# Attention stages of a float32 pipeline: normalisation and all later stages one slot later

## Chip, cores and metric

One NeuronCore of a Trainium2 chip runs the kernel. The metric is the time of one execution on the device, in microseconds (us). The engines go by their short names: PE (TensorE), PEld (its weight loads), DVE (VectorE), ACT (ScalarE), POOL (GpSimd), SP (SyncE, here a queue of DMA issues). Each executes its own instructions in order and waits on semaphores for the others.

## The reference

Attention in chunks, then two gated feed-forward blocks without a nonlinearity, all in float32:

```python
for c in range(nc):                                  # 24 chunks of 32 queries
    k_full = concat(mem_k, k[l_start:r_end])         # 8 memory keys + 16 left, 32, 8 right
    scores = scale * q_c @ k_full.T
    a = exp(scores - max(scores))
    a = a / (sum(a) + 1e-9)
    out[c] = a @ concat(mem_v, v[l_start:r_end])
x = out.reshape(3072, 512)
x = ((x @ w1) * (x @ w2) @ w3) @ w_out               # 512 -> 1024 -> 512
return (x @ w_a) * (x @ w_b) @ w_out2                # 512 -> 1536 -> 512
```

There are 4 batches, 8 heads, 768 positions and a head size of 64. The weights arrive as 64-bit numbers and are turned into float32 on the chip.

## The kernel before

**Phases.** The program has three phases. Up to about 107 us (the weight phase), PE multiplies w3 by w_out once (tile `wps`), while ACT scales and DVE assembles each weight block from its 64-bit halves: `w_scale` (L361, L362 on ACT), then `w_bits` (L366, L367, L368 on DVE; tiles `w3f`, `wo_f`, `dec`). Up to about 560 us (the main loop) PE runs the first block over six tiles of 512 tokens: `psA`, `psB` (x times w1 and w2), then `psY`. After that comes the second block in a form with seven products (`ps`, `ops`). A float32 operand of a large product is split in a high and a low part (L140 on ACT writes the high, L143 on DVE the low one).

**Attention** runs beside the first two phases, in 64 units of 96 queries and 4 heads. A unit passes through eight stages: `a_scores` (PE, tile `sc` in PSUM), `a_max` (DVE: masking or the row maximum, L182, and its negation, L183; from unit 22 on L186 and L190, which also read `sc` from PSUM), `a_exp` (ACT, four exponentials with their sums, L205), `a_norm` (DVE L216 and L217 for the reciprocal of the sums, then POOL L218, the product in place in `t`), `a_trans` (PE, tile `pt`), `a_pt` (ACT L230), `a_pv` (PE, `xp`, for two units at once), `a_x` (ACT L140 and DVE L143 into `xt`, the x of the main loop).

**The order** is written by hand. A slot is a call of `attn_slot`; each unit starts three slots after the last. `STAGES` gives each stage its slot after the unit's start and the order within a slot. Behind the stages of a slot the q and k of a later unit are loaded by SP (`a_load`), and for units from 22 on split (`a_prep_hi` on ACT, `a_prep_lo` on DVE). In the weight phase the slots stand between the products, together with `w_step`, which puts a weight block through one step on ACT and DVE and issues the next load on SP. In the main loop `between` (L627) issues slots after each group of 12 products, so many that `NEED[ti]` slots are done when tile ti begins; `NEED` is the slot count by which the x of a tile is complete. SP's queue therefore holds weight loads (`raw`) and q, k and v loads in one line; a weight load waits until DVE has read the block that had its buffer.

Of the kernel before, what the change touches and what calls it, by code (L numbers as in the profile page):

```python
# [17 lines left out]
GQ = 96  # L18
# [3 lines left out]
TT = 512  # L22
NT1 = B * S // TT
NU = B * NG * 2
# [20 lines left out]
def tile_attention_moe(  # L45
# [204 lines left out]
    def a_x(u):  # L250
# [18 lines left out]


    STAGES = (
        (8, a_x),
        (7, a_pv),
        (6, a_pt),
        (5, a_trans),
        (3, a_norm),
        (2, a_exp),
        (1, a_max),
        (0, a_scores),
    )  # L280
    acount = [-3]
    NSLOT = 3 * (NU - 1) + 9

    NEED = [3 * (2 * -(-TT * (i + 1) // GQ) - 1) + 9 for i in range(NT1)]

    def attn_slot(n=1):
        for _ in range(n):
            s = acount[0]
            if s >= NSLOT:
                return  # L290
            acount[0] += 1
            for off, stage_of in STAGES:
                u, r = divmod(s - off, 3)
                if r == 0 and 0 <= u < NU:
                    stage_of(u)

            if s % 3 == 0 and s // 3 + 1 > NPLAIN + 1:
                a_prep_lo(s // 3 + 1)
            if s % 3 == 2 and s // 3 + 2 > NPLAIN + 1:
                a_prep_hi(s // 3 + 2)  # L300
            if s % 3 == 0 and NPLAIN <= s // 3 + 1 <= NPLAIN + 1:
                a_prep_hi(s // 3 + 1)
            if s % 3 == 1 and NPLAIN <= s // 3 + 1 <= NPLAIN + 1:
                a_prep_lo(s // 3 + 1)
            if s % 3 == 2:
                if s // 3 + 2 <= NPLAIN + 1:
                    a_load(s // 3 + 2)
                if s // 3 + 3 >= NPLAIN + 2:
                    a_load(s // 3 + 3)
            if s % 3 == 1 and s // 3 > 2:  # L310
                a_v(s // 3 - 1)
# [315 lines left out]
    def between():  # L627
# [10 lines left out]
        if ti < NT1 - 1:  # L638
            b = nstep[0] - NB * ti
            attn_slot(NEED[ti] + (NEED[ti + 1] - NEED[ti]) * b // NB - acount[0])  # L640

# [49 lines left out]
    for ti in range(NT1):  # L691
        last = ti == NT1 - 1
        gs = {}
        attn_slot(NEED[ti] - acount[0])
        if last:
# [18 lines left out]
        for n in (0, 2, 1, 3) if last else range(KD):  # L714
            psY = psd.tile([P, 512], F32, tag="d", name="psY")
            i = 0
# [284 lines left out]
```

## Time and profile before

| | us |
|---|---|
| median of 3 runs | 1130.52 |
| lowest and highest run | 1129.53, 1133.06 |
| span of the profiled execution, first to last instruction | 1132.1 |
| PE busy | 1098.0 |
| DVE busy | 647.7 |
| ACT busy | 516.5 |
| POOL busy | 286.1 |

The profiled execution leaves no time of its own beside its span, which is 1.6 us above the median of the runs. Busy times are of that execution. PE is the engine to watch: the other engines matter where PE waits for them. A wait of PE is printed in brackets behind the instruction that ended it, with the releaser that the profile infers.

### The profile page before, as it was taken

To read this page: it belongs to the slowest core of one execution; us is meant where nothing else is said; L and a number is where in the kernel's file an instruction comes from. 1 tells how busy PE (TensorE), PEld (TensorE's weight loads), DVE (VectorE), ACT (ScalarE), POOL (GpSimd) and SP (SyncE) were. 2 spreads that over 40 slices of the span, in tenths; PEclk is the share of its full clock that TensorE was granted. 3 is DMA by queue.
4 is the path that set the end of the run, shared out by engine and by line. 5 is a ranking of instruction groups with operands and counts; after the bars stand their busy time and mean duration, and the time that the engine had idled before them with its cause. 6 is when DMAs were issued, how large, how long until landed. Compare 5 with 4: busy or idle time off the path is not lost.

```text
span 1132.1 us, 15601 instructions
## 1 busy us (share of the span) xinstructions
PE 1098.0 (97%) x5344; PEld 876.0 (77%) x5344; DVE 647.7 (57%) x1374; ACT 516.5 (46%) x1321; POOL 286.1 (25%) x265
## 2 busy tenths in 40 slices
PE   4999999999999999999999999999999999999998
PEld 2555778888787888887887778888888888888887
DVE  5887956887997887874766455253222234232220
ACT  4776755666666666654544443232222223222210
POOL 1111231332332332331204223302223211233210
PEclk9989999999999999999999999999999999999999
DMA  9863535445345445335446553443434451434311
GB/s 276 236 198 124 167 109 162 127 154 173 118 158 178 130 137 188 125 105 196 166 177 219 214 191 149 171 136 134 164 130 148 177 176 66 167 134 182 140 38 37
DMA packets 65540, 174.78 MB, mean 154 GB/s; under 512 B 8152, under 2 KB 20726, under 8 KB 60854
## 3 DMA queue, kind: packets, MB, share of 16 engines
q1 hardware_dynamic: 54647, 107.45, 29.2%
q0 software_dynamic: 10528, 66.08, 15.8%
q8 instruction: 42, 0.69, 0.2%
q14 instruction: 36, 0.29, 0.1%
q10 hardware_dynamic: 287, 0.27, 0.1%
HBM read 140.20 MB, written 33.55 MB: 153 GB/s over the span
## 4 chain that ended last, share of the span: by engine, by line
PE 81%; DVE 3%; issue 2%; ACT 2%; DMA 1%; POOL 1%; DVEq 0%; ACTq 0%; POOLq 0%; SPq 0%
PE ps L787 29%; PE ops L93 17%; PE psA L93 11%; PE psB L93 10%; PE psY L93 10%; PE sc L93 2%; PE xp L93 2%; PE pt L226 1%; ACT t L205 1%; POOL t L218 0%; DVE dec L367 0%; DMA wc<-co 0%; DVE dec L368 0%; DMA vraw<-in_vw 0%; DVE xt L143 0%
## 5 line engine op out<-in xcount | busy, mean ns | idle before, releaser
L787 PE MATMUL ps<-x,w 128*128 128x512 f32 x1512 | 349.5, 390 | 3.2 <-ACT tmp L799 3.2
L787 PEld LDWEIGHTS ps<-x,w 128*128 128x128 f32 x1512 | 283.4, 188 | 64.0 <-ACT tmp L799 5.3
L804 DVE TENSOR_TENSOR tmp<-ps,tmp 128x512 f32<-128x512 f32 x108 | 74.6, 691 | 245.4 <-PE ps L787 241.3
L93 PE MATMUL psA<-xt,w 128*128 128x512 f32 x576 | 145.6, 400 | 2.8 <-ACT xt L140 1.9
L93 PE MATMUL psB<-xt,w 128*128 128x512 f32 x576 | 141.0, 393 | 0.0
L93 PE MATMUL psY<-g,wo 128*128 128x512 f32 x576 | 139.0, 393 | 0.0
L218 POOL TENSOR_TENSOR t<-t,sm 96x512 f32<-96x512 f32 x64 | 81.6, 1275 | 214.5 <-DVE sm L217 116.9
L686 POOL DMA_DIRECT2D w<-wc x72 | 39.5, 552 | 368.4 <-PE ps L787 368.3
L799 ACT ACTIVATE tmp<-ps 128x512 f32<-128x512 f32 x108 | 64.6, 598 | 147.2 <-PE ps L787 119.4
L93 PEld LDWEIGHTS psA<-xt,w 128*128 128x128 f32 x576 | 106.2, 189 | 27.4 <-ACT xt L140 3.1
L93 PEld LDWEIGHTS psY<-g,wo 128*128 128x128 f32 x576 | 105.6, 188 | 21.0
L93 PEld LDWEIGHTS psB<-xt,w 128*128 128x128 f32 x576 | 105.5, 188 | 21.0
L93 PE MATMUL ops<-wo,g 128*128 128x512 f32 x504 | 118.6, 389 | 0.0
L621 POOL TENSOR_TENSOR g<-gv,g 128x512 fp32r<-128x512 f32 x48 | 67.9, 1414 | 190.6 <-ACT g L620 171.8
L93 PEld LDWEIGHTS ops<-wo,g 128*128 128x128 f32 x504 | 94.6, 188 | 19.6
L810 ACT ACTIVATE g<-tmp 128x512 fp32r<-128x512 f32 x66 | 40.7, 633 | 130.1 <-DVE tmp L809 130.1
L811 POOL TENSOR_TENSOR g<-tmp,g 128x512 fp32r<-128x512 f32 x66 | 87.4, 1339 | 26.6 <-ACT g L810 25.7
L93 PE MATMUL wps<-wo_f,w3f 128*128 128x512 f32 x128 | 66.0, 649 | 10.3 <-DVE wo_f L368 10.3
L205 ACT ACTIVATE t<-t,mx 96x128 f32<-96x128 f32 x168 | 65.0, 390 | 14.7 <-DVE mx L190 14.7
L93 PE MATMUL ops<-fo,g 128*128 128x512 f32 x288 | 68.2, 389 | 0.0
L620 ACT ACTIVATE g<-gv 128x512 fp32r<-128x512 f32 x48 | 30.2, 629 | 71.4 <-DVE gv L619 71.4
L93 PEld LDWEIGHTS ops<-fo,g 128*128 128x128 f32 x288 | 54.1, 188 | 11.2
(79 smaller groups left out, 1298.8 us busy)
## 6 DMA issues: line engine op xcount, KB each, us to landing
w<-wc POOLq DMA_DIRECT2D x36, 1024.0 KB, 6.6
w<-wc POOLq DMA_DIRECT2D x36, 768.0 KB, 4.6
wc<-co SPq DMA_DIRECT2D x84, 256.0 KB, 2.5
raw<-in_wab SPq DMA_DIRECT2D x24, 512.0 KB, 3.6
kraw<-in_kt SPq DMA_DIRECT2D x42, 256.0 KB, 2.9
raw<-in_w3a SPq DMA_DIRECT2D x16, 512.0 KB, 8.3
vraw<-in_vw SPq DMA_DIRECT2D x64, 128.0 KB, 3.2
raw<-in_w SPq DMA_DIRECT2D x16, 512.0 KB, 3.4
```

The source lines that it names most:

```text
L93: nc.tensor.matmul(o, lhsT=l, rhs=r, start=first, stop=last)
L205: nc.scalar.activation(t[:, h, :], src[:, h, :], AF.Exp, bias=mx[:, h : h + 1], scale=scale, accum_out=sm[:, h : h + 1],)
L218: nc.gpsimd.tensor_tensor(t, t, sm[:, :, None].to_broadcast([GQ, HH, KW]), ALU.mult)
L226: nc.tensor.transpose(pt[:, h, :], t[:, h, :], id_sb)
L620: nc.scalar.activation(g2[:, 0, :], gv, AF.Copy)
L621: nc.gpsimd.tensor_tensor(g2[:, 1, :], gv, g2[:, 0, :].bitcast(F32), ALU.subtract)
L686: nc.gpsimd.dma_start(out=t[:, c0:c1].bitcast(F32), in_=src[:, c0:c1])
L787: nc.tensor.matmul(ps, lhsT=w[:, i, a, k, :], rhs=xs[i][:, b, k, :], start=first and n == 0, stop=n == 5, skip_group_check=not first,)
L799: nc.scalar.activation(z, ps, AF.Copy)
L804: nc.vector.tensor_tensor(z, ps, y, ALU.add)
L810: nc.scalar.activation(g2[:, 0, :], z, AF.Copy)
L811: nc.gpsimd.tensor_tensor(g2[:, 1, :], z, g2[:, 0, :].bitcast(F32), ALU.subtract)
```

## The change

Five of the eight stages get a slot number that is one higher: x 9, PV 8, the copy of the transposes 7, the transposes 6 and normalisation 4. Exponentials, masking and scores keep 2, 1 and 0. Slots that are equal modulo 3 meet in one slot, so normalisation of a unit now stands directly ahead of the masking of the next one (it stood ahead of the next unit's scores, a slot earlier), the transposes ahead of the scores, and x in the slot after the exponentials, no longer ahead of them in the same slot. The total of slots and `NEED` grow by one.

```diff
     STAGES = (
-        (8, a_x),
...
+        (9, a_x),
...
-        (3, a_norm),
+        (4, a_norm),
         (2, a_exp),
...
-    NSLOT = 3 * (NU - 1) + 9
+    NSLOT = 3 * (NU - 1) + 10
...
-    NEED = [3 * (2 * -(-TT * (i + 1) // GQ) - 1) + 9 for i in range(NT1)]
+    NEED = [3 * (2 * -(-TT * (i + 1) // GQ) - 1) + 10 for i in range(NT1)]
```

On DVE in the weight phase, around the normalisation of unit 0 (`sm_204`) and the masking of unit 1 (`mx_242`), before:

```order
L366 TENSOR_SCALAR w3f_216<-raw64_148 128x512
L367 SCALAR_TENSOR_TENSOR w3f_216<-raw64_148,w3f_216 128x512
L368 ISA w3f_216<-raw64_148,w3f_216 128x1024
L216 TENSOR_SCALAR sm_204<-sm_204 96x4
L217 RECIPROCAL sm_204<-sm_204 96x4
L366 TENSOR_SCALAR wo_f_150<-raw64_156 128x512
L367 SCALAR_TENSOR_TENSOR wo_f_150<-raw64_156,wo_f_150 128x512
L368 ISA wo_f_150<-raw64_156,wo_f_150 128x1024
L182 TENSOR_REDUCE mx_242<-sc_227 96x4
L183 TENSOR_SCALAR mx_242<-mx_242 96x4
```

and in the change, where `sc_224` is the same scores tile:

```order
L366 TENSOR_SCALAR wo_f_150<-raw64_156 128x512
L367 SCALAR_TENSOR_TENSOR wo_f_150<-raw64_156,wo_f_150 128x512
L368 ISA wo_f_150<-raw64_156,wo_f_150 128x1024
L216 TENSOR_SCALAR sm_204<-sm_204 96x4
L217 RECIPROCAL sm_204<-sm_204 96x4
L182 TENSOR_REDUCE mx_242<-sc_224 96x4
L183 TENSOR_SCALAR mx_242<-mx_242 96x4
```

The reciprocal, which releases POOL's product, has moved behind a weight block and directly ahead of the masking.

On ACT in the weight phase, around the exponentials of unit 3 and the first x (`xt`), before and in the change:

```order
L230 ACTIVATE p2_314<-pt_293 128x384
L361 ACTIVATE raw64_222<-raw64_222 128x512
L362 ACTIVATE raw64_222<-raw64_222 128x512
L140 ACTIVATE xt_349<-xp_333 128x4x96
L205 ACTIVATE t_342,sm_344<-sc_319,mx_343 96x128 x4
L361 ACTIVATE raw64_239<-raw64_239 128x512
L362 ACTIVATE raw64_239<-raw64_239 128x512
```

```order
L230 ACTIVATE p2_328<-pt_309 128x384
L205 ACTIVATE t_333,sm_335<-sc_314,mx_334 96x128 x4
L361 ACTIVATE raw64_236<-raw64_236 128x512
L362 ACTIVATE raw64_236<-raw64_236 128x512
L140 ACTIVATE xt_365<-xp_340 128x4x96
```

The high part of x has moved behind the exponentials and a pair of scalings. On DVE its low part (L143) has moved with it, from directly behind the masking of unit 3 to behind one more `w3f` block; for the second x it stands directly behind the masking in both.

On PE at the step into the main loop, before and in the change (`xp_878` and `xp_908` are units 10 and 11):

```order
L93 MATMUL xp_878<-p2_866,vraw_827 64x96 x4
L93 MATMUL wps_552<-wo_f_280,w3f_687 128x512
L93 MATMUL wps_552<-wo_f_280,w3f_730 128x512
L93 MATMUL wps_553<-wo_f_280,w3f_687 128x512
L93 MATMUL wps_553<-wo_f_280,w3f_730 128x512
L226 MATMUL pt_922<-id_sb_101,t_822 128x96 x4
L93 MATMUL psA_935<-xt_349,w12_685 128x512 x12
```

```order
L93 MATMUL wps_548<-wo_f_275,w3f_678 128x512
L93 MATMUL wps_548<-wo_f_275,w3f_730 128x512
L93 MATMUL xp_908<-p2_817,vraw_764 64x96 x4
L93 MATMUL xp_908<-p2_873,vraw_827 64x96 x4
L226 MATMUL pt_929<-id_sb_101,t_822 128x96 x4
L93 MATMUL sc_934<-kraw_105,qraw_103 96x128 x4
L93 MATMUL psA_940<-xt_365,w12_676 128x512 x12
```

PV has moved behind the last `wps` products, and the scores of unit 14 have come ahead of the first `psA`.

## Rows read from the trace of the kernel before

**Rows 1.** The page, part 1: busy us, share of the span, instructions.

```profile
PE 1098.0 (97%) x5344; PEld 876.0 (77%) x5344; DVE 647.7 (57%) x1374; ACT 516.5 (46%) x1321; POOL 286.1 (25%) x265
```

**Rows 2.** PE's waits: us in total, times, longest; the last row for 107 to 525 us alone.

```profile
PE pt L226 <- POOL t L218: 8.5, 4, 5.5
...
PE xp L93 <- DMA vraw<-in_vw: 1.9, 2, 1.3
PE psA L93 <- ACT xt L140: 1.9, 3, 0.7
...
PE pt L226 <- POOL t L218: 2.9, 3, 2.0
```

**Rows 3.** Table by stretch: stretch, its us, busy us by engine, PE clock, DMA share, GB/s.

```profile
24.00:31.00 7.00, 4.37 (x8) 1.76 (x8) 6.41 (x15) 5.06 (x18) 1.17 (x1) 0.52 1.02 285
...
70.00:79.00 9.00, 6.34 (x42) 3.67 (x40) 8.35 (x17) 7.96 (x26) 1.04 (x1) 1.00 0.52 166
79.00:86.00 7.00, 7.00 (x15) 3.95 (x16) 4.04 (x11) 1.50 (x8) 2.08 (x2) 0.52 0.73 179
...
154.00:158.00 4.00, 4.00 (x15) 3.23 (x15) 0.34 (x2) 1.62 (x5) 2.27 (x2) 0.57 0.34 134
```

**Rows 4.** PE's timeline: start us, duration us, instruction; in brackets idle us before it.

```profile
31.41 1.09 PE L93 MATMUL sc<-kraw,qraw 67*96 67x128 f32 x8 [0.45 <-DVE wo_f L366]
...
71.05 1.09 PE L93 MATMUL sc<-kraw,qraw 67*96 67x128 f32 x8 [0.61 <-DVE dec L367]
...
78.95 1.99 PE L93 MATMUL sc<-kraw,qraw 67*96 67x128 f32 x8 [2.04 <-DVE w3f L368]
...
107.38 0.50 PE L93 MATMUL psA<-xt,w 128*128 128x512 f32 x1 [0.52 <-ACT xt L140]
108.13 2.83 PE L93 MATMUL psA<-xt,w 128*128 128x512 f32 x11 [0.25 <-DVE xt L143]
...
152.50 0.55 PE L226 MATMUL pt<-id_sb,t 96*128 96x96 f32 x4 [2.00 <-POOL t L218]
```

**Rows 5.** SP's timeline around 70 us: start, time in the queue, issue.

```profile
69.99 4.08 SPq L349 DMA_DIRECT2D raw<-in_w  x2
74.16 0.47 SPq L124 DMA_DIRECT2D kraw<-in_kt  x1
```

**Rows 6.** DVE's groups by shape, 22 to 80 us: busy us, mean ns, idle before.

```profile
L367 DVE SCALAR_TENSOR_TENSOR w3f<-raw,w3f 128x512 uint32<-128x512 uint32 x12 | 9.0, 753 | 0.4
...
L367 DVE SCALAR_TENSOR_TENSOR wo_f<-raw,wo_f 128x512 uint32<-128x512 uint32 x5 | 7.0, 1409 | 0.2
...
L366 DVE TENSOR_SCALAR wo_f<-raw 128x512 uint32<-128x512 uint32 x5 | 2.1, 424 | 0.1
...
L367 DVE SCALAR_TENSOR_TENSOR dec<-raw,dec 128x512 uint32<-128x512 uint32 x2 | 1.4, 694 | 0.1
```

**Rows 7.** DVE's timeline: the negation alone (28.54) and beside POOL's product (67.52).

```profile
28.54 0.17 DVE L183 TENSOR_SCALAR mx<-mx 96x4 f32<-96x4 f32 x1
...
67.52 0.62 DVE L183 TENSOR_SCALAR mx<-mx 96x4 f32<-96x4 f32 x1
```

**Rows 8.** Timeline of DVE and ACT: end of a block, a scaling, x, a norm.

```profile
29.91 0.69 DVE L368 CUSTOM_DVE_ANT_0 w3f<-raw,w3f 128x1024 uint16<-128x1024 uint16 x1
...
30.19 0.67 ACT L361 ACTIVATE raw<-raw 128x512 f32<-128x512 f32 x1
...
51.56 0.49 ACT L140 ACTIVATE xt<-xp 128x384 fp32r<-128x384 f32 x1 [1.05 <-PE xp L93]
...
53.70 0.17 DVE L216 TENSOR_SCALAR sm<-sm 96x4 f32<-96x4 f32 x1 [1.05 <-ACT t L205]
```

**Rows 9.** The chain that ended last, 118 us: the exponentials of one unit.

```profile
118.24 1.38 ACT t L205 x8
```

**Rows 10.** DVE's groups by shape, 190 to 500 us: splits of q and of x.

```profile
L143 DVE TENSOR_TENSOR q<-qraw,q 64x384 fp32r<-64x384 f32 x40 | 45.0, 1124 | 1.2
...
L143 DVE TENSOR_TENSOR xt<-xp,xt 128x384 fp32r<-128x384 f32 x17 | 9.4, 552 | 6.3 <-ACT xt L140 6.3
```

More of the change, by code (lines that the diff above doesn't have):

```diff
@@ L271, in tile_attention_moe @@
     STAGES = (
-        (8, a_x),
-        (7, a_pv),
-        (6, a_pt),
-        (5, a_trans),
-        (3, a_norm),
+        (9, a_x),
+        (8, a_pv),
+        (7, a_pt),
+        (6, a_trans),
+        (4, a_norm),
         (2, a_exp),
```

## The prediction

> **What bounds it now.** I read the busy times first: TensorE is busy 97% of the span [rows 1], so a microsecond is won or lost only where TensorE waits or where its clock falls. The list of TensorE's waits comes next [rows 2]: transposes (pt) waiting for GpSimd's normalisation 8.5 us in four places, 5.5 of them at once; the products with V (xp) waiting for a transfer 1.9; the first projections (psA) waiting for x 1.9. Of the transposes' 8.5 us only 2.9 lie in the main loop. The table by stretch [rows 3] adds the clock: 0.52 of full speed in 24 to 31 us, again in 79 to 86, and 0.57 in 154 to 158, so 1.2 GHz, half of 2.4, nearly throughout; each time right behind a wait of 2 us or more. At half speed 79 to 86 costs 7 x 0.48 = 3.4 us and 154 to 158 costs 4 x 0.43 = 1.7. The single waits stand in TensorE's timeline [rows 4].
>
> Two of these are not what the bracket says. The scores (sc) at 31.41, 71.05 and 78.95 need only their q and k transfers and a masking finished long before, so a DVE weight block "releases" them by coincidence. The q and k transfers are issued by SP behind weight loads, and those wait for DVE to give a raw buffer back: at 70 us two weight loads hold the queue for 4.1 us, and k of unit 10 is issued at 74.16 [rows 5]. So in the weight phase **DVE's pace sets when TensorE gets its scores.**
>
> **The change, part by part.** No instruction is added or removed.
>
> *Start.* The first transposes now stand behind two products more, and their normalisation behind one more weight block (L366 to L368, 0.42 + 0.69 + 0.69 = 1.8 us [rows 6, 8]). TensorE fills part of its 5.5 us [rows 2] and then waits about 1.8 us longer; the scores at 31.41 [rows 4] wait for transfers in either case. I take 0. Bounds: not below 0, since those transfers set the time; +1.5, if the clock, 0.5 until about 31 us, comes back 3 us later.
>
> *Weight phase, DVE.* Removed: GpSimd's product now starts while DVE masks from PSUM, not while it runs L367 from SBUF. L367 took 1.41 us on five wo_f blocks and 0.69 on the dec blocks [rows 6]; the mean of 0.753 over twelve w3f blocks is eleven of 0.69 and one more of 1.4. Six such holds go: -6 x 0.72 = -4.3. Added: the negation L183 right behind the masking now falls in GpSimd's time. It takes 0.62 us there and 0.17 alone [rows 7]. Units 1 to 7 get this, 7 x 0.45 = +3.2; from unit 8 on it stood so before.
>
> Added too: waits on ScalarE. Freed of the hold, DVE reaches its next block when L368 ends, 30.60, but ScalarE's scaling of that block follows the exponentials and ends at 30.86 [rows 8]: 0.26 us, three times, +0.8. And x moves. Before, ScalarE split x ahead of the exponentials; now it does so behind them, while DVE's half of x stands early in DVE's queue and holds the weight blocks behind it. First time: exponentials 1.38 [rows 9], two scalings of 0.67, x 0.49 [rows 8] make 3.2 us, against one block of 1.8 that DVE has to do meanwhile: +1.4. Second: DVE has nothing between masking and x and waits 1.38 + 0.49 = 1.9, where it waited 1.05 for the same exponentials before [rows 8, 9]: +0.85. Third: 1.9 against 1.8, +0.1.
>
> Sum for DVE at the block that frees the buffer for unit 10: -4.3 + 3.2 + 0.8 + 1.4 + 0.85 + 0.1 = **+2.0 us**. SP issues q and k that much later, and TensorE, which waits there already, starts these scores at 81 instead of 78.95. Bounds: -1.2 if ScalarE never makes DVE wait (only the holds count), +4.2 if half of the removed holds return on the block behind the negation. I take 2.0; the order decides the waits, and the durations are all shown.
>
> Here the Trainium skill has a rule (SBUF — State Buffer, Who interferes with whom): VectorE and GpSimd share one pair of SBUF ports as an exclusive lock, a tensor_reduce never contends for it, and a tensor_scalar can. The trace agrees with it in the 1.41 against 0.69 and in the 0.62 against 0.17. By that rule alone this step is a gain, the -1.2 of the lower bound; by the order of the queues it is +2.0.
>
> *Step into the main loop.* x of unit 11 now precedes transposes and scores of unit 14, all ahead of the first psA; before, TensorE went from the transposes straight to psA and lost 0.52 + 0.25 [rows 4]. The scores (about 1 us) now cover x: -0.77. Between 0 and that.
>
> *Main loop.* The total of attention slots rises by one, so norm, transposes, PV and x keep their places between the products, and scores, masking and exponentials come one slot earlier. The sums that DVE had to wait for are there. From unit 22 on the product ran beside the split of q: 1.12 us for 384 columns, 40 times, against 0.55 for x of the same width [rows 10], 23 us of DVE. Now it runs beside a masking that reads PSUM. DVE isn't the bound there, so this only ends late transposes: 2.9 - 2.0 = 0.9, and one psA wait of 0.7 [rows 2]: -1.6. The 2.0 us at 152.5 [rows 4] I leave: DVE is as full as before up to there, and as many rows stand ahead of that norm. Bounds: 0, and -5.3 if it goes too, with the 1.7 of clock behind it.
>
> All else (600 us of products after the last unit) keeps its instructions.
>
> **Sum:** 0 + 2.0 - 0.8 - 1.6 = -0.4 us. The profiled execution spans 1132.1, which gives 1131.7; its span is 1.6 above the median of the runs, 1130.52. From the median: **1130.1 us**.
>
> **Rivals.**
> (a) *Faster: the release of DVE carries through.* If ScalarE runs ahead enough, SP is served earlier, the waits of 0.61 and 2.04 [rows 4] go, and the clock stays up in 79 to 86: -2.65 - 3.4, with -0.8 and -1.6 of the other steps: -8.4, 1122.1. For it: DVE is busy 8.35 of 9 us in 70 to 79 [rows 3], so any gain counts. Against it: the order puts ScalarE's x behind its exponentials on three occasions. Half of it would give 1126.
> (b) *Slower: a second fall of the clock.* Scores of unit 9 wait 0.61 us at 71 because of the same SP queue; with DVE 2.0 late they wait 2.6. It decides at about 2 us: the waits of 2.04 and 2.00 were followed by half speed, the xp wait of 1.3 [rows 2] wasn't. One more stretch as in 79 to 86 costs 3.4, and the start's 1.5 is likely with it, since nothing then absorbs it: -0.4 + 4.9 = +4.5, 1135.0. Against it: the slow stretch would then stand ahead of unit 10's wait and run partly inside it. The Trainium skill (TensorE: Matmul & The Clock Gate, HAM oscillation) says that gaps put the array back to its lower clock and that each return is paid anew; the trace agrees in its three falls, with 0.52, 0.52 and 0.57.
> (c) *The change does little of what it says.* From unit 8 to 13 norm already stood directly ahead of the masking on DVE; if seven units don't matter, the time stays at 1130.5.
>
> **How the numbers follow.** Forecast 0.42, (c) 0.08, (a) 0.25, (b) 0.25. About 0.3%, 3.4 us, is what a measurement of this kernel can tell from no change. Forecast and (c) stay within it (0.50); (a) is faster by more (0.25), (b) slower by more (0.25). The range takes in the forecast with its unknowns (-1.2 to +4.2 for DVE, 0 to -5.3 for the loop), half of (a) and all of (b): 1124.5 to 1136. It leaves out the better half of (a) and a worse (b), 2 in 10. The forecast's own range is 1127 to 1133.5.
>
> **What would show it.** Right: L367 at 0.69 on the wo_f blocks; L183 near 0.6 from unit 1; DVE idle before L143 of xt, released by ScalarE, 1.4 and 1.9 us between 40 and 56; SP's k for unit 10 near 76 and its scores near 81; no wait before the first psA; the split of q near 0.55. Wrong: those scores before 78 (then (a)); granted clock about 0.5 between 72 and 79 (then (b)); a new wait of TensorE above 1 us after 200.

## The result, and the profile after

The changed kernel takes 1146.35 us (median of four runs, 1143.94 to 1147.33) against 1130.07 before: 1.0132 of it, interval 1.0113 to 1.0152, slower by some 15 us. The forecast was 1130.1 with a range up to 1136. The profiled execution of the change is its fastest (span 1142.2); that of before was the slowest of its runs (1132.1). The traces therefore show 10 of the 16 us between the medians; the rest belongs to executions without a trace.

The page, part 1, of the change answers to [rows 1]:

```profile
PE 1097.6 (96%) x5344; PEld 877.5 (77%) x5344; DVE 617.1 (54%) x1374; ACT 518.0 (45%) x1321; POOL 271.3 (24%) x265
```

DVE works 30.6 us less than before, and yet TensorE finishes later. Its waits in the main loop (107 to 525 us) say where, beside 2.9 and 1.9 in [rows 2]:

```profile
PE pt L226 <- POOL t L218: 10.7, 10, 3.4
PE psA L93 <- ACT xt L140: 1.1, 1, 1.1
PE psY L93 <- POOL g L621: 1.0, 1, 1.0
```

The waits one by one, from PE's timeline (start, duration, instruction, idle before it). The first five answer to [rows 4], the last five are new:

```profile
30.55 1.99 PE L93 MATMUL sc<-kraw,qraw 67*96 67x128 f32 x8 [1.88 <-DMA qraw<-in_qt]
...
72.17 1.08 PE L93 MATMUL sc<-kraw,qraw 67*96 67x128 f32 x8 [1.00 <-DMA qraw<-in_qt]
...
79.80 1.08 PE L93 MATMUL sc<-kraw,qraw 67*96 67x128 f32 x8 [1.83 <-DMA qraw<-in_qt]
...
106.36 1.08 PE L93 MATMUL sc<-kraw,qraw 67*96 67x128 f32 x8 [1.10 <-DMA qraw<-in_qt]
...
151.35 0.90 PE L226 MATMUL pt<-id_sb,t 96*128 96x96 f32 x4 [3.36 <-POOL t L218]
...
299.58 0.55 PE L226 MATMUL pt<-id_sb,t 96*128 96x96 f32 x4 [2.89 <-POOL t L218]
...
330.29 0.55 PE L226 MATMUL pt<-id_sb,t 96*128 96x96 f32 x4 [1.42 <-POOL t L218]
338.24 0.55 PE L226 MATMUL pt<-id_sb,t 96*128 96x96 f32 x4 [0.64 <-POOL t L218]
345.71 0.73 PE L93 MATMUL psY<-g,wo 128*128 128x512 f32 x2 [1.02 <-POOL g L621]
347.76 0.55 PE L226 MATMUL pt<-id_sb,t 96*128 96x96 f32 x4 [1.31 <-POOL t L218]
```

Behind 160 us all but one of the waits above 0.5 us that are new lie between 290 and 348 us, in the third of the six tiles of the main loop. In the table below a tile's time runs from the moment its first psA could have started to the same point of the next tile (from PE's timeline), and "idle" is the sum of PE's waits in the third tile.

| kernel | first psA | tile 1 | 2 | **3** | 4 | 5 | 6 | idle in 3 |
|---|---|---|---|---|---|---|---|---|
| before | 106.9 | 89.1 | 79.9 | **83.7** | 80.5 | 78.4 | 66.3 | 0.95 |
| change | 107.2 | 89.1 | 80.5 | **94.6** | 79.5 | 77.5 | 66.4 | 7.8 |

The third tile lost 10.9 us; everything else together gained 0.8. Idle time is 6.9 of it. Much of the rest is the clock, which fell to half twice there (table by stretch; the column behind POOL is PE's granted clock):

```profile
300.00:304.00 4.00, 4.00 (x15) 3.27 (x14) 2.59 (x6) 2.35 (x9) 0.00 (x0) 0.61 0.01 4
...
347.00:352.00 5.00, 4.24 (x16) 3.52 (x17) 3.52 (x16) 3.75 (x13) 0.70 (x1) 0.67 0.12 42
```

That is 4 x 0.39 + 5 x 0.33 = 3.2 us, each time behind a wait of PE.

**What is special about the third tile.** `NEED` is 42, 72, 102, 138, 168, 198 in the kernel before. Most tiles have 30 slots for 24 gaps between groups of 12 products, and which slots share a gap rotates. The third has 36 for 24: one slot behind psA, two behind psB, the same way all through, and a unit is three slots. The totals modulo 3 decide which. Before (remainder 0) the slots 1 and 2 modulo 3 shared the gap behind psB; with totals one higher (remainder 1) the slots 2 and 0 do, and slot 1 stands alone behind psA. The third tile also has the least time for a unit: 12 units, 6.8 us each when undisturbed (81.6 / 12, e5 below), against 7.9 elsewhere (78.5 / 10).

### The profile page after: what moved, and what is told of

It is laid out like the page before. It is cut to its first block, busy times and chain, and to the rows that moved or that the text cites. A ratio compares the mean times of both kernels' runs of the same rounds, so it can differ in the third digit from the quotient of the medians.

```text
span 1142.2 us, 15548 instructions
## 1 busy us (share of the span) xinstructions
PE 1097.6 (96%) x5344; PEld 877.5 (77%) x5344; DVE 617.1 (54%) x1374; ACT 518.0 (45%) x1321; POOL 271.3 (24%) x265
## 4 chain that ended last, share of the span: by engine, by line
PE 72%; DVE 6%; ACT 4%; issue 3%; POOL 1%; DMA 1%; SPq 0%; DVEq 0%; ACTq 0%; POOLq 0%
PE ps L787 29%; PE ops L93 17%; PE psY L93 9%; PE psA L93 7%; PE psB L93 7%; ACT t L205 1%; PE sc L93 1%; PE pt L226 1%; PE xp L93 1%; DVE dec L368 1%; DMA wc<-co 1%; DVE gv L619 1%; POOL g L621 1%; DVE dec L367 1%; DVE t L186 1%
## 5 line engine op out<-in xcount | busy, mean ns | idle before, releaser
L804 DVE TENSOR_TENSOR tmp<-ps,tmp 128x512 f32<-128x512 f32 x108 | 74.6, 691 | 245.3 <-PE ps L787 241.3
L218 POOL TENSOR_TENSOR t<-t,sm 96x512 f32<-96x512 f32 x64 | 68.3, 1068 | 230.2 <-DVE sm L217 192.9
L621 POOL TENSOR_TENSOR g<-gv,g 128x512 fp32r<-128x512 f32 x48 | 66.2, 1380 | 199.6 <-ACT g L620 199.6
L93 PEld LDWEIGHTS ops<-wo,g 128*128 128x128 f32 x504 | 94.6, 188 | 19.7
L93 PE MATMUL wps<-wo_f,w3f 128*128 128x512 f32 x128 | 61.5, 621 | 11.6 <-DVE wo_f L368 10.5
```

What stands on the lines that cost most here:

```text
L93: nc.tensor.matmul(o, lhsT=l, rhs=r, start=first, stop=last)
L218: nc.gpsimd.tensor_tensor(t, t, sm[:, :, None].to_broadcast([GQ, HH, KW]), ALU.mult)
L621: nc.gpsimd.tensor_tensor(g2[:, 1, :], gv, g2[:, 0, :].bitcast(F32), ALU.subtract)
L804: nc.vector.tensor_tensor(z, ps, y, ALU.add)
```

## The experiments

Ratios are to the kernel before, with their 95% intervals. In the expectations, T1, T2, T3, S and L are the theories. The first suspect was x. DVE's groups of the change from 190 to 500 us, as in [rows 10], have 31.7 us of idle time ahead of the low half of x where 6.3 stood (the last two numbers are idle time and its releaser), while the split of q has become short:

```profile
L143 DVE TENSOR_TENSOR q<-qraw,q 64x384 fp32r<-64x384 f32 x38 | 22.0, 578 | 1.0
...
L143 DVE TENSOR_TENSOR xt<-xp,xt 128x384 fp32r<-128x384 f32 x17 | 9.5, 558 | 31.7 <-ACT xt L140 31.7
```

### First: x, and the splits of k and q

**e1**, of the stages x alone, in the kernel before (with both totals at 10):

```diff
-        (8, a_x),
+        (9, a_x),
```

> The kernel before with x alone moved, from 8 to 9, so that ScalarE's half of x stands behind the exponentials and the splits of k and q, as in the change; normalisation, transposes and PV keep their slots. T1 (DVE's half of x waits for ScalarE at the head of DVE's queue and holds normalisation behind it): most of the loss is here already, 1138 to 1146 us; DVE waits for ScalarE's x some 50 us in the main loop where before had 18, and the transposes wait for GpSimd more than 6 us there (before 2.9). T2 (the low parts of k and q, now ahead of normalisation on DVE, make it late): no loss, 1128 to 1132 us, since normalisation still stands ahead of them here. T3 (scores, masking and exponentials come a slot earlier against the products, and that alone decides): the same shift is here, 1140 to 1146 us, with no longer waits of DVE for x.

1162.19 us, ratio 1.0271 (1.0248 to 1.0294): worse than the whole change and than any theory said. The third tile takes 101.8 us. Its totals are those of e7 below (1144.90 us), against which x behind the exponentials costs 17 us more. PE's waits show a new entry at their head, the scores waiting for the masking:

```profile
PE sc L93 <- DVE mx L190: 11.0, 6, 3.7
```

**e2**, in the change: DVE's half of x becomes a stage of its own, one slot behind ScalarE's and last in `STAGES`; the totals are 11.

```diff
         for src, dst in parts:
             split_hi(dst[:, 0], src)
-        for src, dst in parts:
+        xlo[u] = parts
+
+    def a_x_lo(u):
+        for src, dst in xlo.pop(u, ()):
             split_lo(dst[:, 1], src, dst[:, 0])
...
         (0, a_scores),
+        (10, a_x_lo),
```

> The change with DVE's half of x put a slot later than ScalarE's half, behind normalisation and masking (slots 10; the totals one higher). T1: the loss goes, 1129 to 1134 us; the waits of DVE for ScalarE's x in the main loop fall from 55 us to under 10 and the transposes wait under 4 us there. T2: the loss stays, 1142 to 1147 us, with the waits of DVE for ScalarE's k still above 20 us. T3: stays, 1142 to 1147 us.

1138.42 us, 1.0056 (1.0037 to 1.0075): between the two. In the third tile (87.1) no transpose waits any more. Instead the first psA of five tiles waits for DVE's x, which now stands in the last slot ahead of it:

```profile
PE psA L93 <- DVE xt L144: 8.9, 5, 2.1
```

**e3**, the low parts of k and q behind normalisation, in the change:

```diff
-            if s % 3 == 0 and s // 3 + 1 > NPLAIN + 1:
+            if s % 3 == 1 and s // 3 + 1 > NPLAIN + 1:
                 a_prep_lo(s // 3 + 1)
```

> The change with the low parts of k and q put a slot later, behind normalisation and masking. T2: the loss goes, 1129 to 1134 us, and the transposes wait under 4 us in the main loop. T1: most of it stays, 1140 to 1147 us: DVE's half of x still stands ahead of normalisation. T3: stays, 1142 to 1147 us.

1138.95 us, 1.0063 (1.0048 to 1.0078): again between. Third tile 84.8. So x and the splits each undo most of the third tile's loss, which neither theory has.

**e4**, the change for units 0 to 11 only; the moved stages of later units, and `NEED` from its second entry on, are as before:

```diff
             for off, stage_of in STAGES:
-                u, r = divmod(s - off, 3)
-                if r == 0 and 0 <= u < NU:
-                    stage_of(u)
+                for late in (1, 0):
+                    u, r = divmod(s - off + (off > 2 and not late), 3)
+                    if r == 0 and 0 <= u < NU and (off < 3) <= late and (off < 3 or late == (u < 12)):
+                        stage_of(u)
```

> The change for units 0 to 11 alone; from unit 12 on the stages keep their old slots. All three theories put the loss in the main loop: 1129 to 1132 us here, with the first psA near 107 us and the main loop as long as before. If the weight phase has a part in the 16 us that separate the medians (the profiled executions are only 10 apart), this is slower: 1134 us or more.

1130.66 us, 0.9992 (0.9980 to 1.0005): no loss from the change in the weight phase. Third tile 83.7. In its trace the first psA starts at 110.9 us, not near 107 as expected, and a first tile of 83.9 us (before 89.1) makes up for it.

### Second: spare slots

**e5** is e2 with totals 12, **e6** the change with x at 11 and totals 12, **e7** the kernel before with nothing but totals 10, **e8** is e2 and e3 together with totals 12. The edits of e7, and that of x in e6:

```diff
-    NSLOT = 3 * (NU - 1) + 9
+    NSLOT = 3 * (NU - 1) + 10
...
-    NEED = [3 * (2 * -(-TT * (i + 1) // GQ) - 1) + 9 for i in range(NT1)]
+    NEED = [3 * (2 * -(-TT * (i + 1) // GQ) - 1) + 10 for i in range(NT1)]
```

```diff
-        (9, a_x),
+        (11, a_x),
```

> The change with DVE's half of x a slot later, behind normalisation (as in e2), and one spare slot: the totals at 12 instead of 11, so that x of a tile is not in the last slot ahead of its first product. T1 (x at the head of DVE's queue is the whole loss; what e2 still lost, 6.5 us, are its five waits of psA for DVE's half of x, 8.9 us in all): 1128 to 1133 us, psA waits under 3 us, transposes wait under 2 us. T2 (the low parts of k and q ahead of normalisation have a part of their own): 1135 to 1140 us, with waits of transposes back.

> The change with x two slots later still (11, totals 12), so that ScalarE's half stands ahead of the exponentials again; the low parts of k and q stay ahead of normalisation. T1: the loss goes, 1128 to 1133 us; DVE's waits for x in the main loop fall from 55 us to some 20, as before. T2: about half stays, 1136 to 1141 us, with the transposes waiting 4 us or more in the main loop.

> The kernel before with its old slots and only the totals one higher (10 instead of 9): every stage one slot earlier against the products of the main loop, and x of a tile no longer in the last slot ahead of it. T3 (the shift of scores, masking and exponentials against the products costs by itself): 1136 us or more. T1 and T2: no loss, 1127 to 1132 us; the waits of psA for x (2.1 us in five places before) should go, which could give 1 to 2 us.

> Both cures at once with the spare slot: DVE's half of x and the low parts of k and q behind normalisation and masking, totals 12. T1 and T2 alike: 1126 to 1132 us. Against e5 it tells what the low parts of k and q add: under 2 us by T1, 4 us or more by T2. If both e5 and e8 stay above 1135 us, neither theory is the cause.

| | us | ratio | third tile |
|---|---|---|---|
| e5 | 1121.20 | 0.9916 (0.9898 to 0.9934) | 81.6 |
| e6 | 1122.69 | 0.9918 (0.9902 to 0.9933) | 82.4 |
| e7 | 1144.90 | 1.0116 (1.0098 to 1.0134) | 93.4 |
| e8 | 1122.41 | 0.9917 (0.9901 to 0.9932) | 81.6 |

e7 is the turning point: no stage changed its slot number, and the third tile lost 9.7 us. Its scores wait for the masking in seven places:

```profile
PE sc L93 <- DVE mx L190: 9.0, 7, 2.2
```

T1 and T2 gave no loss here and fall as the whole cause. T3 gave a loss, but e5, e6 and e8 shift the stages further and are faster than both kernels, and than any theory had said. What they share with the kernel before is a total divisible by 3. The theory that was formed from this, L, is in the next expectation.

### Third: the remainder

The edits are those of e7 with other numbers: **e9** is the change with totals 12, **e10** with totals 13, **e11** the kernel before with totals 12, **e12** is e5 with totals 13.

> The change, its stages untouched, with the totals at 12 instead of 10. L (a closed loop of DVE and ScalarE: masking, exponentials, splits of k and q, normalisation, next masking; what decides is whether the block from the raw halves and gv stand between masking and the first instruction that waits for ScalarE, or behind it; that hangs on which two slots share a gap between products, so on the totals modulo 3, and bites only in the third tile, which has 36 slots for 24 gaps): 1119 to 1125 us, the third tile near 82 us instead of 94.6. T1 (x at the head of DVE's queue, whatever the totals): 1140 us or more, third tile above 90 us. S (it is only the spare slots ahead of a tile that help): also 1119 to 1125 us; it parts from L in the next kernel.

> The change with the totals at 13: three spare slots, but the same remainder modulo 3 as the change itself. L: the loss is back, 1138 to 1148 us, third tile above 90 us. S: 1119 to 1125 us. T1: 1140 us or more, as in every kernel that keeps the change's order.

> The kernel before with the totals at 12 instead of 9: three spare slots, the same remainder as before. L: 1126 to 1132 us, third tile 82 to 84 us (before 83.7), where one slot more alone (e7) gave 93.4. T3 (any shift of the stages against the products costs): 1140 us or more.

> e5 (DVE's half of x behind normalisation) with the totals at 13 instead of 12, the change's remainder. L: slower than e5 by 5 to 15 us, 1126 to 1137 us, since gv and the block stand in the loop again; the third tile 86 to 92 us against 81.6, without the extra for x. T1: as e5, 1119 to 1124 us. S: as e5.

| | remainder | us | ratio | third tile |
|---|---|---|---|---|
| e9 | 0 | 1128.34 | 0.9979 (0.9967 to 0.9990) | 85.4 |
| e10 | 1 | 1138.67 | 1.0069 (1.0045 to 1.0092) | 93.6 |
| e11 | 0 | 1131.88 | 1.0006 (0.9992 to 1.0021) | 84.0 |
| e12 | 1 | 1129.82 | 0.9990 (0.9974 to 1.0006) | 86.8 |

For stages in one order, the remainder decides over the third tile, not the spare slots: the change itself has one of 85.4 with totals 12, and 93.6 with 13. In time e10 is 10.3 us above e9. But the spare slots count in the time too: e10 is 7.7 us below the change with the same remainder, and in its trace tiles 2, 4, 5 and 6 are about 1 to 2 us shorter each. In the kernel before they gave nothing (e11). S falls as the whole cause with e10, and T1 with e9. L has the sign of all four; for e9 it was 3 us too hopeful, in the time as in the tile. e12 against e10 shows that x is one part of it: out of the loop, at the same remainder, it is worth 6.8 us of the tile.

**The loop in the trace.** DVE's timeline in the third tile, first of the change (idle before an instruction in brackets; the four L190 of a masking are cut to the first):

```profile
327.45 0.16 DVE L216 TENSOR_SCALAR sm<-sm 96x4 f32<-96x4 f32 x1
...
327.74 0.67 DVE L186 TENSOR_TENSOR t<-sc,mask_sb 96x512 f32<-96x512 f32 x1
328.44 0.29 DVE L190 CUSTOM_DVE_ANT_0 t<-sc,t 96x128 f32<-96x128 f32 x1
...
331.93 0.69 DVE L143 TENSOR_TENSOR k<-kraw,k 128x512 fp32r<-128x512 f32 x1 [2.56 <-ACT k L140]
332.65 0.55 DVE L143 TENSOR_TENSOR q<-qraw,q 64x384 fp32r<-64x384 f32 x1
333.24 0.69 DVE L619 TENSOR_TENSOR gv<-psB,av 128x512 f32<-128x512 f32 x1
333.84 0.42 DVE L366 TENSOR_SCALAR dec<-raw 128x512 uint32<-128x512 uint32 x1
334.30 0.69 DVE L367 SCALAR_TENSOR_TENSOR dec<-raw,dec 128x512 uint32<-128x512 uint32 x1
335.02 1.68 DVE L368 CUSTOM_DVE_ANT_0 dec<-raw,dec 128x1024 uint16<-128x1024 uint16 x1
336.62 0.15 DVE L216 TENSOR_SCALAR sm<-sm 96x4 f32<-96x4 f32 x1
```

and of e9, the same stages with totals 12:

```profile
325.80 0.17 DVE L216 TENSOR_SCALAR sm<-sm 96x4 f32<-96x4 f32 x1
...
326.10 0.67 DVE L186 TENSOR_TENSOR t<-sc,mask_sb 96x512 f32<-96x512 f32 x1
326.81 0.29 DVE L190 CUSTOM_DVE_ANT_0 t<-sc,t 96x128 f32<-96x128 f32 x1
...
327.65 0.68 DVE L619 TENSOR_TENSOR gv<-psB,av 128x512 f32<-128x512 f32 x1
328.26 0.41 DVE L366 TENSOR_SCALAR dec<-raw 128x512 uint32<-128x512 uint32 x1
328.71 0.69 DVE L367 SCALAR_TENSOR_TENSOR dec<-raw,dec 128x512 uint32<-128x512 uint32 x1
329.54 0.69 DVE L368 CUSTOM_DVE_ANT_0 dec<-raw,dec 128x1024 uint16<-128x1024 uint16 x1
330.14 0.68 DVE L143 TENSOR_TENSOR k<-kraw,k 128x512 fp32r<-128x512 f32 x1
...
332.77 0.16 DVE L216 TENSOR_SCALAR sm<-sm 96x4 f32<-96x4 f32 x1
```

The masking releases ScalarE's exponentials, and behind them ScalarE writes the high part of k (and x). DVE's low part of k waits for that; normalisation and the next masking stand behind it, and the masking releases the next exponentials. In e9, gv (DVE's product of psA and psB, L619) and the weight block (L366 to L368) lie between masking and k and use the time: from one normalisation to the next 6.97 us, no idle time. In the change they lie behind k. DVE first idles for 2.56 us and then does the same work: 9.17 us, where 6.8 are to be had. (In each of the two, one instruction runs beside POOL's L621 and takes about 1 us longer than its like elsewhere: L368 1.68 here, the split of q 1.53 in e9.) These are two periods of a tile; over all of it they scatter from 5.6 to 9.8 us in the change (mean 7.9) and from 4.9 to 9.5 in e9 (mean 7.3). PE's transposes wait for normalisation in six of the twelve units, before in two and in e9 in none.

In e7, as in the kernel before, normalisation stands ahead of the splits and is the first on DVE to wait for ScalarE. Before, gv and a block lie between masking and normalisation, which at 335.15 us does not wait. In e7 they lie behind the splits, ahead of the next masking:

```profile
332.43 0.17 DVE L216 TENSOR_SCALAR sm<-sm 96x4 f32<-96x4 f32 x1 [1.94 <-ACT t L205]
...
334.99 0.69 DVE L619 TENSOR_TENSOR gv<-psB,av 128x512 f32<-128x512 f32 x1
...
338.37 0.67 DVE L186 TENSOR_TENSOR t<-sc,mask_sb 96x512 f32<-96x512 f32 x1
```

So the masking is late there, and PE's scores wait for it.

### Fourth: pieces of the loop, and the tile alone

**e13**, in the change, issues the slots of a gap ahead of the step of the weight blocks:

```diff
     def between():
         nstep[0] += 1
+        if ti < NT1 - 1:
+            b = nstep[0] - NB * ti
+            attn_slot(NEED[ti] + (NEED[ti + 1] - NEED[ti]) * b // NB - acount[0])
         if nplan[0] < len(plan):
...
-        if ti < NT1 - 1:
-            b = nstep[0] - NB * ti
-            attn_slot(NEED[ti] + (NEED[ti + 1] - NEED[ti]) * b // NB - acount[0])
```

> The change with one thing exchanged in the gaps of the main loop: the slots are issued ahead of the step of the weight blocks, not behind it; totals 10, every stage in its slot. L (the loop masking, exponentials, split of k, normalisation, next masking sets the pace in the third tile; the change took some 7.9 us a unit, 9.5 with x, where 6.8 are to be had): the block of 1.8 to 2.8 us then falls into the time of the exponentials, and ScalarE's two scalings of 1.2 us leave the loop as well: third tile 83 to 88 us instead of 94.6, time 1133 to 1139 us. If it is the shared gap as such (the place of the slots against the products, not what stands between masking and the splits): third tile above 92 us, 1143 us or more.

Third tile 84.0 us, as L said, with no stage, slot or total changed. The time, 1150.74 us (1.0190, 1.0175 to 1.0205), missed L's 1133 to 1139, and the other theory has the time but not the tile: tiles 1, 2, 4 and 5 became 2.5 to 5.0 us longer each than in the change. In the stretch read there (229 to 242 us), ScalarE's scalings and copies of the blocks stand between the halves of a unit in another way, and DVE waits 3.55 us for x; that this is all of it was not tested.

**e14** moves gv alone:

```diff
         ab_half(psB, w, 1, rhs)
-        between()
         nc.vector.tensor_tensor(gv, psB[:, :TT], av, ALU.mult)
+        between()
```

> The change with gv (the product of psA and psB on DVE, 0.69 us) issued ahead of the slots of its gap instead of behind them; nothing else moves, totals 10. L: gv falls into the time of the exponentials, some 0.7 us of loop for each of 12 units: third tile 84 to 89 us, 1135 to 1141 us. If it is the shared gap as such: no change, third tile above 92 us, 1143 us or more. Worse than the change (1148 us or more) if DVE, which now waits for the end of psB there, is the later of the two.

Third tile 91.1, 3.4 us less than the change where L said 6 to 11; time 1156.49 us (1.0229, 1.0208 to 1.0250), the bad case of the expectation. DVE waits at gv for the end of psB, 39.5 us between 107 and 570 us where the change has 20.9, and holds everything behind it:

```profile
DVE gv L618 <- PE psB L93: 39.5, 18, 5.3
```

**e15**, the change with the shift of e9 at the start and the end of the third tile alone:

```diff
-    NEED = [3 * (2 * -(-TT * (i + 1) // GQ) - 1) + 10 for i in range(NT1)]
+    NEED = [3 * (2 * -(-TT * (i + 1) // GQ) - 1) + (12 if i in (2, 3) else 10) for i in range(NT1)]
```

> The change with the totals at 12 for the start and the end of the third tile alone and 10 elsewhere. L: the loss lies in the third tile: 84 to 87 us there instead of 94.6 and 1134 to 1139 us in all, that is 8 to 11 us below the change; the rest to e9's 1128 lies in other tiles. If the other tiles carry as much: 1141 us or more.

Third tile 84.9, as expected. Time 1142.07 us (1.0101, 1.0084 to 1.0118), only 4 below the change: the second tile, which now has two slots more (32), took 84.1 instead of 80.5, and the fourth, with two fewer (28), 81.2 instead of 79.5. The loss is cured where it arose, and about half of it comes up again in the neighbouring tiles. That the second loses because it has to issue more is a reading; why the fourth loses stays open.

## Why the prediction was wrong

**The start: at its upper bound, not at 0.** Transposes and scores together wait 4.44 + 1.88 us (before 5.53 + 0.45), nearly the same. But the granted clock is 0.50 between 28 and 34 us, where before it was so between 26 and 30, and PE starts its first PV at 39.95 us instead of 38.81 with the same products behind it. That is the case for which the text gave +1.5. The other traces lean the same way: 38.9 to 42.3 us in the twelve with the change's order at the start, 37.5 to 40.4 in the three with the old one (e1, e7, e11).

**DVE in the weight phase: right in kind, the sum 0.8 too high.** DVE's groups from 22 to 80 us show that the hold is gone, as on [rows 6]:

```profile
L367 DVE SCALAR_TENSOR_TENSOR w3f<-raw,w3f 128x512 uint32<-128x512 uint32 x12 | 8.3, 693 | 0.4
...
L367 DVE SCALAR_TENSOR_TENSOR wo_f<-raw,wo_f 128x512 uint32<-128x512 uint32 x5 | 3.5, 693 | 0.2
```

L183 takes 0.62 us beside the product, as taken from [rows 7], but in five of the seven units; in the other two the masking waits 0.39 us for its scores, and L183 stays at 0.17. DVE waits for ScalarE's scaling four times, 1.2 us in all, where 0.8 stood. Its waits for x, forecast at 1.4 and 1.9 us, are 1.25 and 2.02:

```profile
42.37 0.56 DVE L143 TENSOR_TENSOR xt<-xp,xt 128x384 fp32r<-128x384 f32 x1 [1.25 <-ACT xt L140]
...
53.95 0.56 DVE L143 TENSOR_TENSOR xt<-xp,xt 128x384 fp32r<-128x384 f32 x1 [2.02 <-ACT xt L140]
```

SP issues k of unit 10 at 75.40 instead of 74.16 [rows 5]:

```profile
75.40 0.47 SPq L124 DMA_DIRECT2D kraw<-in_kt  x1
```

That is +1.24 where 2.0 stood; the scores start at 79.80, forecast 81. What was not forecast: in this trace the clock stays up there, which gives 3.4 us (the last section shows that this is no property of the change), and later waits of PE for q at 85.77 and 106.36 (1.11 and 1.10 us) and others take them back. The phase ends at 107.2, before 106.9. One trace of each does not carry so small a difference: in the five kernels with the same order up to there (e3, e4, e13, e14, e15) it ends between 106.7 and 110.9 us.

**The step into the main loop: right for psA, without the gain.** The first psA waits for nothing. The scores ahead of it wait 1.10 us for a transfer, so the -0.77 is not seen in the time.

**The main loop: the step that failed.** It said: "The total of attention slots rises by one, so norm, transposes, PV and x keep their places between the products, and scores, masking and exponentials come one slot earlier. The sums that DVE had to wait for are there", and from that -1.6 us. Measured: +9.7 us from the first to the last psY (168.7 to 594.5 against 168.5 to 584.6), and 10.9 us in the third tile alone. The premise on contention held in the main: the split of q takes 0.58 us for 1.12 in [rows 10], while that of k went from 0.74 to 0.85. The Trainium skill (SBUF — State Buffer, Who interferes with whom) describes a pair of ports that VectorE and GpSimd share as an exclusive lock. The 0.58 against 1.12 agrees with it in direction. But DVE's own work did not set the pace; a loop through ScalarE did. From 277 to 371 us, the third tile, DVE is busy 63.7 of 94 us; the same 204 instructions took 74.6 of 84 before. Two things were not worked out. First, what the one slot does to the gaps: in the third tile it changes the partner of every slot, and e7 shows that this alone costs 9.7 us there. Second, what then stands on DVE between the masking and the first instruction that waits for ScalarE. "DVE isn't the bound there" stands without a row; DVE had idle time because it waited inside the loop, and "only ends late transposes" did not ask what DVE would wait for next. The 6 us between the medians that the two traces don't show stay open.

**The stall at 152.5** stayed, as said, and grew from 2.00 to 3.36 us. The first tile takes 89.1 us in both.

**The rivals.** (b) named a slower result by a second fall of the clock near 72 to 79 us. The sign came true, the mechanism didn't: the clock is 1.00 there, and its new falls in the main loop lie in the third tile, behind waits that the loop made. That it "decides at about 2 us" of wait did not hold over the runs either (last section). (a) and (c) are out. The sign on record that the text set against itself, "a new wait of TensorE above 1 us after 200", is what the trace shows, four times.

**What the change is worth with its totals at 12.** e9 is 0.21% faster than before, about 2.6 us. In tiles without waits the new order is quicker: 78.55 us for the second tile (e9, e10, e12) against 79.9 before, and 79.15 in e11. With transposes and scores next to each other the products are interrupted 14 times in that tile instead of 21. How much of the 0.6 to 1.4 us comes from this was not separated. **e5, at 1121.2 us, beats both kernels.** It has no wait of PE left in tiles 2 to 6.

## What to carry to other kernels

Where stages are issued in slots between groups of work, count slots per gap before moving anything: if a stretch has a fixed ratio that fits the unit's period, one slot more in a total changes which stages share a gap for all of it, and costs as much as a reordering (here 9.7 us for a "+1"). For each engine pair that hands work back and forth, write down the closed loop (masking, exponentials, split, normalisation, next masking) with its durations from the trace, and compare its period with the time a unit has at the tightest stretch; work that doesn't wait belongs between the release and the wait. Then measure the whole: e13 and e14 made the third tile shorter and the kernel slower. An engine's low busy share doesn't show slack if its idle time lies inside such a loop.

## What the chip showed beside that

The clock did not fall in the change between 70 and 86 us, though PE waited 1.00 us at 72.17 and 1.83 at 79.80; before, it stood at 0.52 in 79 to 86 [rows 3] behind waits of 0.61 and 2.04. The granted clock of the change:

```profile
70.00:79.00 9.00, 6.97 (x42) 3.79 (x40) 8.45 (x17) 8.03 (x27) 1.04 (x1) 1.00 0.59 189
79.00:86.00 7.00, 5.08 (x22) 2.99 (x23) 5.43 (x13) 3.40 (x13) 2.07 (x2) 1.00 0.69 171
```

Waits of nearly the same length thus had different prices, 3.4 us or none, in the same place. It is not the change that keeps the clock up: of the traces with its stages, e3, e9 and e15 have a fall between 72 and 92 us, and e10, e13 and e14 have none. Nor does the length of the wait sort them: e15 has a fall behind 1.43 us, e2 none behind 2.54. From PE's timeline and the table by stretch, first e15, then e2:

```profile
88.03 1.09 PE L93 MATMUL sc<-kraw,qraw 67*96 67x128 f32 x8 [1.43 <-DMA qraw<-in_qt]
88.00:92.00 4.00, 3.98 (x12) 2.24 (x13) 2.75 (x6) 1.23 (x3) 0.00 (x0) 0.63 0.03 7
...
79.94 1.08 PE L93 MATMUL sc<-kraw,qraw 67*96 67x128 f32 x8 [2.54 <-DMA qraw<-in_qt]
79.00:86.00 7.00, 4.85 (x20) 2.73 (x20) 4.97 (x13) 3.11 (x12) 1.78 (x2) 1.00 0.71 172
```

What else decides was not looked into. DVE's busy time fell by 30.6 us, 23.0 of it at the split of q between 190 and 500 us, and the kernel got slower: time taken from an engine is a gain only where another one waits for it.
